# Block 0 of a sliding-window attention layer: output products moved between the score visits, buffers reassigned, one LayerNorm step later

## The chip, the cores and the metric

The kernel runs on one core of a Trainium2 chip. The metric is the device time of one execution in microseconds (us). The core's engines are TensorE (PE in the profile; its weight loads are PEld), VectorE (DVE), ScalarE (ACT), GpSimd (POOL) and SyncE (SP), which here issues the DMAs. Each engine runs its own instructions in order; they meet through semaphores.

## The reference

One layer of a transformer over 2048 rows of 1024 columns, in bf16: a LayerNorm, causal attention with 32 heads of 32 columns in which a query sees itself and the 255 rows ahead of it, an output projection with a residual, a second LayerNorm, and a feed-forward part of width 3584 with a residual.

```python
qkv = (x @ wqkv).reshape(B, S, 3, H, Dh) ...
scores = jnp.einsum("bhqd,bhkd->bhqk", q, k) * (Dh ** -0.5)
mask = (idx[:, None] - idx[None, :] >= 0) & (idx[:, None] - idx[None, :] < W)   # W = 256
p = _softmax(jnp.where(mask[None, None], scores, -1e9), axis=-1)
o = jnp.einsum("bhqk,bhkd->bhqd", p, v) ... @ wo
h = x + _A_ref(_layernorm(x), wqkv, wo)
h2 = h + silu(_layernorm(h) @ w1) @ w2
```

## The kernel before, in words

The rows are cut into four blocks of 512. TensorE's dense work is a list of groups of 8 matmuls of 128 x 512: for each block 8 groups for v and 16 for q and k (four heads share one group of 128 columns), then 32 groups of the output projection (`wo_group`), then the feed-forward part. A group accumulates in one of three PSUM banks taken in turn (`next_acc`; `bank0` to `bank2`), and VectorE (for some early groups ScalarE) copies the result out with one CAST, `L266` for q and k, `L256` for v.

The attention's small work is threaded into this dense work. `Attention.between` is called ahead of every dense matmul and counts them in `seen`; a number such as 108 below is such a position, "the matmul before which something is put". From the first q group of block 0 (position 0) to the end of the output projection the kernel keeps two tables by position:

- A **visit** (`visit_0` for block 0, `visit` for the later ones) is a burst of some 30 to 50 small score matmuls (`L377`). The scores of one unit of four heads go to `sc`, a PSUM tile of four banks. The scores of one to three further heads of neighbouring units go to single banks beside it, which the code calls `idle` (the bank of the next dense group), `out` (the fourth bank, `bank3`) and `behind` (the bank of the dense group before, which must have been copied out by then). ScalarE then takes the exponentials, the single banks first and in the order of the code, `sc` last (`L426` and `L435` in block 0; `L318`, `L324` and `L325` later), and writes them to SBUF; GpSimd zeroes the masked triangles in place (`select`, `L446`), and in block 0 copies one 64-column strip from a unit to its neighbour (`join_0`, `L408`).
- A **piece** (`attn_piece`) is the product of these exponentials with v for two of a group's four heads: 18 matmuls in block 0, 24 later (`L456`), into `bank3`, the same bank that a visit calls `out`. VectorE then divides by the row sums (`attn_norm`: a reciprocal at `L467` and a multiplication at `L468`). After a group's second piece a DMA transpose of the result is put on the SP queue (`attn_transpose`, by `run_late` ahead of the next dense group).

Block 0 has 16 units, numbered m = 2i + odd for group of heads i; piece (i, pair) reads units 2i and 2i+1 for two heads. Its ten visits stand at positions 84, 108, 132, 148, ... 244; from there on a visit of the later blocks stands at every 16th position, 260, 276, 292 and so on. Visits come in threes: the first holds four heads of a unit and three of the next, the second four of a unit and heads of two others, the third four of a unit and the last two heads of its neighbour.

The exponentials of block 0 lie in one SBUF tile, `r_e`, of 13312 columns. A unit needs 2560 columns, 640 a head. There are five places for units: Z (column 0), A (3072), B (5632), C (8192) and D (10752). Later blocks use the same columns: the first 3072 as a ring for the corner chunks (`c_ring`), A and C for `xbuf`, B and D for `ybuf` of even and odd groups. In those a head has 512 columns of triangles and 128 of a middle chunk, the middles of four heads behind the triangles. A place may be written again only after the pieces that read it.

Next to that, VectorE does the first LayerNorm of block 1 while block 0's q and k groups run, as a list of steps taken from the front behind each group: four of row statistics, a first guess of the reciprocal root, three Newton rounds (three small instructions each, `L216` to `L218`), then four row-wise normalizations (`L223`) with a DMA transpose (`L227`) for each. How many steps are taken behind which of the 16 groups is a tuple of 16 numbers (line 682). Groups 10 to 15 are copied out by VectorE, so a step behind one group stands ahead of the next group's copy in VectorE's queue. The transposed rows feed block 1's v groups, which begin at position 128.

Lines that the change touches: `POS_0` (41), `chunk_of` (293), `exp_xy` (321), `visit` (332), `visit_0` (410), the tables of `Attention` (485) and the tuple (682).

Of the kernel before, what the change touches and what calls it, by code (L numbers as in the profile page):

```python
# [11 lines left out]
ACT = mybir.ActivationFunctionType  # L12
ALU = mybir.AluOpType

P = 128
# [22 lines left out]
    [(0, "X", 2), (1, "Y", 1), (2, "X", 3)],  # L38
    [(1, "Y", 2), (2, "C", 1), (3, "Y", 3)],
]  # L40
POS_0 = [(0, 3072, 5632, 8192, 10752)["ZABCD".index(c)] for c in "ZDABCDZBADZCADBC"]
PIECE_0 = {"X": (0, 128, 512, 320), "Y": (0, 128, 256, 512)}
FIRST = [
    (0, 0), (1,), (0, 1), (1, 0), (0, 2), (1, 1), (0, 3), (1, 2), (1, 3),
# [5 lines left out]
def kernel(  # L50
# [10 lines left out]
    nc = tc.nc  # L61
# [11 lines left out]
    G = H // 4  # L73
    VW = DH + 1
    scale = float(DH) ** -0.5
# [21 lines left out]
    four = [ps.tile([P, 512], F32, name=f"bank{i}") for i in range(4)]  # L97
# [31 lines left out]
    def xbuf(i):  # L129
        return r_e[:, 3072 + 5120 * (i % 2):5632 + 5120 * (i % 2)]  # L130

    def ybuf(i):
        return r_e[:, 5632 + 5120 * (i % 2):8192 + 5120 * (i % 2)]

    def tri_of(e):
        return e[:, 0:2048].rearrange("p (h c q) -> p h c q", h=4, q=256)

    def full_of(e):
        return e[:, 2048:2560].rearrange("p (h q) -> p h q", q=P)
# [136 lines left out]
    def run_late():  # L276
        while late:
            late.pop(0)()
# [11 lines left out]
            late.append(lambda: nc.sync.dma_start(out=h_dram[(b * 4 + j) * P:(b * 4 + j + 1) * P, :], in_=t_out[j % 2]))  # L290


    def chunk_of(i, bank, piece, h):
        if i >= G and bank == "C":
            return c_ring[:, (i + 1) % 3, h, piece * P:(piece + 1) * P]
        if i >= G:
            c0 = 2048 + h * P if piece == 2 else h * 512 + (piece - piece // 3) * P
        else:
            c0 = POS_0[2 * i + (bank != "X")] + h * 640 + (384 if bank == "C" else PIECE_0[bank][piece])
            return r_e[:, c0:c0 + P]  # L300
        return (xbuf if bank == "X" else ybuf)(i)[:, c0:c0 + P]

    def unit_xy(i, odd):
        q0 = odd * P
        mid, first, last = odd, odd - 2, odd + 2
        return [
            [(i, mid, q0, q0 + 320, 64), (i, last, q0 + 256, q0 + 384, 384), (i, first, q0, q0 + 64, 0)],
            [(i, mid, q0 + 64, q0 + 384, 128), (i, first, q0, q0 + 128, 0), (i, last, q0 + 320, q0 + 384, 448)],
        ]

    def unit_c(i):
        pair = (i, i + 1) if (i + 1) % 3 < (i + 2) % 3 else (i + 1, i)
        return [[(ii, kt, q * P, q * P + P, (n * 2 + m) * P)
                 for n, ii in enumerate(pair) for m, (kt, q) in enumerate(((-1, 0), (2, 3)))]] * 2

    def exp_c(i, h, bank):
        lo, hi = sorted(((i + 1) % 3, (i + 2) % 3))
        nc.scalar.activation(out=c_ring[:, lo:hi + 1:hi - lo, h, :], in_=four[bank].rearrange("p (n q) -> p n q", q=256),  # L318
                             func=ACT.Exp, scale=scale)

    def exp_xy(e, banks, h0, h1):
        tri, mid = banks[:, :, 0:192], banks[:, :, 192:320]
        tri = bass.AP(tensor=tri.tensor, offset=tri.offset, ap=[*tri.ap[:2], [320, 2], tri.ap[2]])
        nc.scalar.activation(out=tri_of(e)[:, h0:h1, :, 64:256], in_=tri, func=ACT.Exp, scale=scale)  # L324
        nc.scalar.activation(out=full_of(e)[:, h0:h1, :], in_=mid, func=ACT.Exp, scale=scale)  # L325

    def select_xy(e, pair):
        four_q = e[:, 1024 * pair:1024 * (pair + 1)].rearrange("p (c q) -> p c q", q=256)
# [3 lines left out]
    def visit(i, n):  # L332


        now = acc_n[0] % 3
        idle, behind, out = (now + 1) % 3, (now + 2) % 3, 3
        if n == 0:
            own, e_own = unit_xy(i, 0), xbuf(i)
            more = [(0, idle, unit_c(i)), (1, out, unit_c(i)), (2, behind, unit_c(i))]
        elif n == 1:  # L340
            own, e_own = unit_xy(i, 1), ybuf(i)
            more = [(3, idle, unit_c(i)), (0, out, unit_xy(i + 1, 0)), (1, behind, unit_xy(i + 1, 0))]
        else:
            own, e_own = unit_xy(i + 1, 1), ybuf(i + 1)
            more = [(2, out, unit_xy(i + 1, 0)), (3, behind, unit_xy(i + 1, 0))]
        scores(own, more, {idle, out} if n == 0 else ())
        side = [h for h, _, unit in more if len(unit[0]) == 3]
        for h, bank, unit in more:
            if h in side:
                exp_xy(xbuf(i + 1), four[bank].rearrange("p (h q) -> p h q", h=1), h, h + 1)  # L350
            else:
                exp_c(i, h, bank)
        if side:
            select_xy(xbuf(i + 1), side[0] // 2)
        exp_xy(e_own, sc[:], 0, 4)
        for pair in range(2):
            select_xy(e_own, pair)
# [34 lines left out]
    def heads_0(m, h0, h1):  # L392
        return r_e[:, POS_0[m] + 640 * h0:POS_0[m] + 640 * h1].rearrange("p (h q) -> p h q", q=640)

    def select_0(m, h0, h1):
        e = heads_0(m, h0, h1)

        if m % 2:
            select(e[:, :, 0:P], e[:, :, 0:P], True)
            select(e[:, :, 512:640], e[:, :, 320:448], True)  # L400
            select(e[:, :, 256:384], e[:, :, 256:384], False)
        else:
            select(e[:, :, 512:640], e[:, :, 256:384], False)
            select(e[:, :, 0:P], e[:, :, 0:P], True)
            select(e[:, :, 320:448], e[:, :, 320:448], True)

    def join_0(m, h0, h1):
        nc.gpsimd.tensor_copy(out=heads_0(m, h0, h1)[:, :, 384:448], in_=heads_0(m - 1, h0, h1)[:, :, 448:512])  # L408

    def visit_0(k):  # L410

        now = acc_n[0] % 3
        idle, behind, out = (now + 1) % 3, (now + 2) % 3, 3
        m, n = k // 3 * 5, k % 3
        if k == 9:
            own, more = m, []
        elif n == 0:
            own, more = m, [(0, idle, m + 1), (1, out, m + 1), (2, behind, m + 1)]
        elif n == 1:
            own, more = m + 2, [(3, idle, m + 1), (0, out, m + 3), (1, behind, m + 3)]  # L420
        else:
            own, more = m + 4, [(2, out, m + 3), (3, behind, m + 3)]
        scores(unit_0(own), [(h, bank, unit_0(mm)) for h, bank, mm in more], (idle, out))
        for h, bank, mm in more:
            at = POS_0[mm] + 640 * h
            nc.scalar.activation(out=r_e[:, at:at + 512], in_=four[bank], func=ACT.Exp, scale=scale)  # L426
        done = []
        for mm in sorted({mm for _, _, mm in more}):
            heads = [h for h, _, x in more if x == mm]
            if mm % 2:  # L430
                done.append((mm, heads[0], heads[-1] + 1))
                select_0(*done[-1])
            elif heads[-1] == 3:
                select_0(mm, 0, 4)
        nc.scalar.activation(out=heads_0(own, 0, 4)[:, :, 0:512], in_=sc[:], func=ACT.Exp, scale=scale)  # L435
        step = 2 if own % 2 else 4
        for h in range(0, 4, step):
            select_0(own, h, h + step)
            if own % 2:
                join_0(own, h, h + step)  # L440
        for mm, h0, h1 in done:
            join_0(mm, h0, h1)
# [42 lines left out]
    class Attention:  # L485


        def __init__(self):
            self.seen = 0
            self.visits, self.pieces = {}, {}  # L490
            at = [84, 108, *range(132, 260, 16)]
            for k in range(10):
                self.visits[at[k]] = lambda k=k: visit_0(k)
            gaps = (1, 6), (2, 6), (2, 10), (3, 7), (4, 6), (4, 10), (5, 6), (5, 10), (6, 6), (6, 10), (7, 7), (8, 6), (8, 10), (9, 7)
            for d, (k, late) in enumerate(gaps):
                self.pieces[at[k] + late] = (d // 2, d % 2)
            self.pieces.update({267: (G - 1, 0), 271: (G - 1, 1)})
            for p in range((NB - 1) * G // 2):
                i, t = G + 2 * p, 256 + 48 * p
                for n in range(3):  # L500
                    self.visits[t + 4 + 16 * n] = lambda i=i, n=n: visit(i, n)
                for n in range(4):
                    self.pieces[t + (41, 46, 59, 76)[n]] = (i + n // 2, n % 2)
# [87 lines left out]
    for n, step in enumerate(FIRST):  # L591
# [24 lines left out]
        elif len(step) == 4:  # L616
            j, k0, k1, _ = step
# [10 lines left out]
    for j in range(2):  # L628
        for c in range(2):
            nc.scalar.activation(out=v[:, j, c * 16:(c + 1) * 16, 0:DH], in_=first[j][c].rearrange("p (h d) -> p h d", d=DH),  # L630
                                 func=ACT.Identity, scale=rs[:, j:j + 1])
# [44 lines left out]
    for g0 in range(0, G, 4):  # L676
        for w in range(2):
            for g in range(g0, g0 + 4):
                run_late()
                n = g0 * 2 + w * 4 + g % 4  # L680
                qk_group(0, w, g, dve if g % 2 or n > 9 else act, stream.between)
                for _ in range((0, 0, 0, 0, 0, 0, 1, 1, 1, 1, 2, 1, 2, 3, 3, 1)[n]):
                    steps.pop(0)()
    assert not steps

# [166 lines left out]
```

## Time and profile before

| | |
|---|---|
| median of 3 runs | 689.88 us (689.15 to 690.59) |
| the profiled execution | 688.68 us, of which the profile's span is 687.0 us |
| PE busy | 673.2 us, 98% of the span |
| DVE, ACT, POOL busy | 296.0, 235.7, 160.9 us |
| granted clock of PE | 1.0 throughout |

The profile's timeline has one row for consecutive instructions of one engine and kind: start, duration, engine, line, operation, output <- input, size and count, and in brackets the idle time of that engine ahead of it with what ended it. Two things help in reading it. Some matmul records are missing; a gap of one dense step (0.216 us) behind a visit is often such a record. And the end of a matmul is modelled, so it is best to go by starts.

### The profile page before, as it was taken

The page shows a single profiled execution, that of the slowest core. Times are in us where ns is not written, and L with a number is a line of the kernel's source. Part 1 is how long each engine was busy: PE and PEld are TensorE (multiplying, and loading weights), DVE is VectorE, ACT ScalarE, POOL GpSimd, SP SyncE. Part 2 cuts the span into 40 slices and gives each one's busy share as a digit, 9 for nine tenths or more (in the row PEclk, how much of TensorE's full clock was granted, in tenths as well). Part 3 has the DMA queues.
Part 4 walks back from the last instruction along what each step waited for, and adds up shares of the span by engine and source line. Part 5 has one row for each costly group of instructions (what it writes and reads, how often), then busy time and mean ns, then how long its engine had stood idle before and what let it go on. Part 6 is the DMA issues. An engine that isn't in the chain of part 4 may idle for free.

```text
span 687.0 us, 14482 instructions
## 1 busy us (share of the span) xinstructions
PE 673.2 (98%) x6097; PEld 338.0 (49%) x6200; DVE 296.0 (43%) x617; ACT 235.7 (34%) x397; POOL 160.9 (23%) x287
## 2 busy tenths in 40 slices
PE   9999999999999999999999999999999999999998
PEld 4445555555555555444444444444444444444445
DVE  5296755774444446743316133342244251343111
ACT  7346666676767674023300033200133100233000
POOL 1046867666676755000000000000000000000000
PEclk9999999999999999999999999999999999999999
DMA  8824144125522788775033310023300123100110
GB/s 275 260 43 107 18 71 94 26 31 109 181 80 71 209 275 224 152 252 188 1 98 110 77 39 1 0 93 77 76 1 0 36 85 87 39 1 0 31 38 24
DMA packets 77616, 61.49 MB, mean 90 GB/s; under 512 B 52464, under 2 KB 60656, under 8 KB 77552
## 3 DMA queue, kind: packets, MB, share of 16 engines
q1 hardware_dynamic: 77408, 60.31, 32.0%
q8 instruction: 48, 0.79, 0.5%
q10 hardware_dynamic: 144, 0.26, 0.1%
q14 instruction: 16, 0.13, 0.1%
HBM read 39.85 MB, written 8.39 MB: 70 GB/s over the span
## 4 chain that ended last, share of the span: by engine, by line
PE 97%; issue 2%; DVE 1%; ACT 0%; ACTq 0%
PE hacc L771 16%; PE hacc L799 15%; PE bank L264 15%; PE bank L799 13%; PE bank L771 12%; PE bank L285 8%; PE bank L254 6%; PE bank L456 5%; PE sc L377 2%; PE bank L377 2%; PE bank L588 1%; PE tp L254 1%; PE bank L188 0%; ACT r_e L324 0%; DVE r_a L266 0%
## 5 line engine op out<-in xcount | busy, mean ns | idle before, releaser
L446 POOL TENSOR_SCALAR_AFFINE_SELECT r_e<-r_e 128x512 bf16<-128x512 bf16 (+2 forms) x264 | 154.3, 598 | 108.6 <-ACT r_e L324 50.8
L799 PEld LDWEIGHTS <-r_a 128*128 128x128 bf16 x952 | 90.8, 98 | 103.0
L771 PEld LDWEIGHTS <-r_w 128*128 128x128 bf16 x896 | 87.6, 98 | 105.8
L799 PE MATMUL hacc<-r_a 128*128 128x512 bf16 (+2 forms) x523 | 103.2, 357 | 0.5
L799 PE MATMUL bank<-r_a 128*128 128x512 bf16 x411 | 91.3, 380 | 0.5
L771 PE MATMUL hacc<-r_e,r_w 128*128 128x512 bf16 x374 | 84.3, 380 | 0.5
L264 PEld LDWEIGHTS <-r_w 128*128 128x128 bf16 x512 | 45.3, 97 | 47.8
L771 PE MATMUL bank<-r_e,r_w 128*128 128x512 bf16 x286 | 64.3, 380 | 0.1
L266 DVE CAST r_a<-bank 128x512 bf16<-128x512 f32 x59 | 40.7, 689 | 48.6 <-PE bank L264 38.9
L264 PE MATMUL bank<-r_t,r_w 128*128 128x512 bf16 x233 | 57.6, 379 | 2.5 <-issue 1.9
L264 PE MATMUL bank<-r_w 128*128 128x512 bf16 x241 | 56.2, 379 | 1.9 <-issue 1.6
L285 PE MATMUL bank<-r_o,r_a 128*128 128x512 bf16 x242 | 56.5, 379 | 1.5 <-issue 1.1
L324 ACT ACTIVATE r_e<-sc 128x1536 bf16<-128x1536 f32 x36 | 53.5, 1485 | 0.0
L456 PEld LDWEIGHTS <-r_e 128*128 128x128 bf16 x1440 | 45.6, 96 | 15.8 <-issue 1.4
L780 ACT ACTIVATE r_n<-bank 128x512 f32<-128x512 f32 x18 | 10.7, 597 | 117.0 <-PE bank L771 117.0
L456 PE MATMUL bank<-r_a,r_e 128*128 128x33 bf16 x1440 | 46.2, 178 | 0.1
L318 ACT ACTIVATE r_e<-bank 128x512 bf16<-128x512 f32 x48 | 26.1, 598 | 43.5 <-PE bank L377 43.5
L780 ACT ACTIVATE r_n<-hacc 128x512 f32<-128x512 f32 x24 | 14.3, 597 | 75.5 <-PE hacc L771 75.5
L814 DVE SCALAR_TENSOR_TENSOR r_t<-bank,r_t 128x512 bf16<-128x512 f32 x15 | 10.3, 685 | 66.6 <-PE bank L799 66.6
L285 PEld LDWEIGHTS <-r_a 128*128 128x128 bf16 x256 | 23.4, 97 | 25.7
L814 DVE SCALAR_TENSOR_TENSOR r_t<-hacc,r_t 128x512 bf16<-128x512 f32 (+2 forms) x19 | 12.0, 633 | 53.8 <-PE hacc L799 48.4
L377 PEld LDWEIGHTS <-r_a 32*64 32x64 bf16 x1856 | 23.9, 104 | 20.8 <-issue 20.0
(98 smaller groups left out, 592.8 us busy)
## 6 DMA issues: line engine op xcount, KB each, us to landing
r_w<-in_B_w_dram SPq DMA_DIRECT2D x8, 896.0 KB, 6.1
r_a<-in_B_w_dram SPq DMA_DIRECT2D x7, 1024.0 KB, 9.9
r_w<-in_A_wqkv_dram SPq DMA_DIRECT2D x4, 1024.0 KB, 8.5
h_dram<-r_t SPq DMA_DIRECT2D x16, 256.0 KB, 2.9
r_t<-h_dram SPq DMA_DIRECT2D x16, 256.0 KB, 3.0
out_dram<-r_t SPq DMA_DIRECT2D x31, 128.0 KB, 1.7
r_e<-h_dram SPq DMA_DIRECT2D x3, 1024.0 KB, 5.8
r_o<-in_A_x_dram SPq DMA_DIRECT2D x11, 256.0 KB, 5.3
```

What stands on the lines that cost most here:

```text
L254: nc.tensor.matmul(acc, lhsT=lnT_b[b % 2][:, kt, j * P:(j + 1) * P], rhs=wv[:, kt, c * 512:(c + 1) * 512], start=(kt == 0), stop=(kt == KT ...
L264: nc.tensor.matmul(acc, lhsT=wqk[:, kt, col0:col0 + P], rhs=lnT_b[b % 2][:, kt, :], start=(kt == 0), stop=(kt == KT - 1))
L266: copy(out=(qT, kT)[which][b][:, g, :], in_=acc)
L285: nc.tensor.matmul(acc, lhsT=qT[b][:, g, j * P:(j + 1) * P], rhs=wo[:, g, c * 512:(c + 1) * 512], start=(g == 0), stop=(g == G - 1))
L318: nc.scalar.activation(out=c_ring[:, lo:hi + 1:hi - lo, h, :], in_=four[bank].rearrange("p (n q) -> p n q", q=256), func=ACT.Exp, scale=scale)
L324: nc.scalar.activation(out=tri_of(e)[:, h0:h1, :, 64:256], in_=tri, func=ACT.Exp, scale=scale)
L377: nc.tensor.matmul(bank[half * 64:half * 64 + 64, col:col + qb - qa], lhsT=kT[t // 4][r0:r0 + DH, g, k0:k0 + 64], rhs=qT[b][r0:r0 + DH, g, ...
L446: nc.gpsimd.affine_select(out=dst, in_=src, pattern=[[0, n] for n in dst.shape[1:-1]] + [[sgn, P]], compare_op=ALU.is_ge if upper else ALU ...
L456: nc.tensor.matmul(o_ps[:, qt * 2 + hh, 0:VW], lhsT=chunk_of(i, bank, piece, pair * 2 + hh), rhs=v[:, b * 4 + kt, g * 4 + pair * 2 + hh, : ...
L771: nc.tensor.matmul(acc, lhsT=w1[:, kt, ft * P:(ft + 1) * P], rhs=ln2T[b][:, kt, :], start=(kt == 0), stop=(kt == KT - 1))
L780: nc.scalar.activation(out=th, in_=acc, func=ACT.Tanh, scale=0.5)
L799: nc.tensor.matmul(acc[:, 0:c1 - c0], lhsT=gT[:, ft, j * P:(j + 1) * P], rhs=w2[ft // 4][:, ft % 4, c0:c1], start=(ft == 0), stop=(ft == F ...
```

## The change

Three things move.

1. **Pieces.** Block 0's pieces get new positions. A visit that is followed by two pieces now has them 5 and 10 positions behind it (before: 6 and 10). The two pieces of group 5, which stood behind two different visits (219 and 234), now both stand behind the visit at 212 (217 and 222); group 6's first piece goes from 238 to 235. The last piece of block 0 goes from 271 to 284, behind the visit at 276. Three others move by one position.
2. **Buffers.** So that these positions find their data and do not overwrite it, units 10, 12, 13, 14 and 15 change places: 10 from Z to B, 12 from A to Z, 13 from D to A, 15 from C to D, and 14 from B to a new place N at column 7936, which covers the end of B and most of C. Since unit 14's last two heads are now still to be read when the visit at 276 has written its exponentials, the middle chunks of an odd group's `xbuf` are stored with heads 2 and 3 first (`mid_at`): what the visit at 276 writes then lies clear of them. In `visit_0`, the join of a unit whose neighbour was finished by an earlier visit is issued directly behind its selects, and no longer behind the selects of the visit's own unit.
3. **Newton rounds.** The tuple of steps takes none behind group 11 and three behind group 12 (before: one and two), so the second of the three Newton rounds moves from behind group 11's copy to behind group 12's.

```diff
-POS_0 = [(0, 3072, 5632, 8192, 10752)["ZABCD".index(c)] for c in "ZDABCDZBADZCADBC"]
+POS_0 = [(0, 3072, 5632, 7936, 8192, 10752)["ZABNCD".index(c)] for c in "ZDABCDZBADBCZAND"]
...
+    def mid_at(i, bank, h):
+        return (h + 2) % 4 if bank == "X" and i % 2 else h
...
-            c0 = 2048 + h * P if piece == 2 else h * 512 + (piece - piece // 3) * P
+            c0 = 2048 + mid_at(i, bank, h) * P if piece == 2 else h * 512 + (piece - piece // 3) * P
...
-    def exp_xy(e, banks, h0, h1):
+    def exp_xy(e, banks, h0, h1, m0=0):
...
-        nc.scalar.activation(out=full_of(e)[:, h0:h1, :], in_=mid, func=ACT.Exp, scale=scale)
+        nc.scalar.activation(out=full_of(e)[:, m0:m0 + h1 - h0, :], in_=mid, func=ACT.Exp, scale=scale)
...
-                exp_xy(xbuf(i + 1), four[bank].rearrange("p (h q) -> p h q", h=1), h, h + 1)
+                exp_xy(xbuf(i + 1), four[bank].rearrange("p (h q) -> p h q", h=1), h, h + 1, mid_at(i + 1, "X", h))
...
-                done.append((mm, heads[0], heads[-1] + 1))
-                select_0(*done[-1])
+                select_0(mm, heads[0], heads[-1] + 1)
+                if own == mm - 1:
+                    done.append((mm, heads[0], heads[-1] + 1))
+                else:
+                    join_0(mm, heads[0], heads[-1] + 1)
...
-            gaps = (1, 6), (2, 6), (2, 10), (3, 7), (4, 6), (4, 10), (5, 6), (5, 10), (6, 6), (6, 10), (7, 7), (8, 6), (8, 10), (9, 7)
+            gaps = (1, 7), (2, 5), (2, 10), (3, 7), (4, 5), (4, 10), (5, 5), (5, 10), (6, 5), (6, 10), (7, 5), (7, 10), (8, 7), (9, 7)
...
-            self.pieces.update({267: (G - 1, 0), 271: (G - 1, 1)})
+            self.pieces.update({267: (G - 1, 0), 284: (G - 1, 1)})
...
-                for _ in range((0, 0, 0, 0, 0, 0, 1, 1, 1, 1, 2, 1, 2, 3, 3, 1)[n]):
+                for _ in range((0, 0, 0, 0, 0, 0, 1, 1, 1, 1, 2, 0, 3, 3, 3, 1)[n]):
```

## The prediction, made blind

> **What bounds the kernel.** I read the page first, then busy time by stretch, then the timeline around block 0's visits.
>
> ```profile
> span 687.0 us, 14482 instructions
> PE 97%; issue 2%; DVE 1%; ACT 0%; ACTq 0%
> ```
> ```profile
> 38.40:112.00 73.60, 71.18 (x1126) 39.51 (x1145) 49.73 (x116) 44.61 (x59) 49.86 (x108) 1.00 0.35 66
> ```
> ```profile
> 326.77 6.91 PE hacc L771 x32
> ```
>
> The first two are the page's span and the shares of the chain that ended last: PE carries it. The third is the stretch of the visits concerned (38.4 to 112 us; columns: length, then busy time and count of PE, PEld, DVE, ACT, POOL, then clock): PE is idle for 2.4 of 73.6 us, and DVE, ACT and POOL are busy for about 60 to 70%. So nothing but PE can be the bound in the mean, and all that a reordering can win here are the moments in which PE waits. The fourth, from the chain, is the undisturbed dense rate: 6.91 / 32 = 0.216 us a step. I use it as a ruler: a place where starts lie further apart than the work between them is a stall. With it I find four kinds.
>
> **Stall 1: the visit at 108.** The timeline around it, and the visit at 212, which has the same make-up:
>
> ```profile
> 43.84 0.15 DVE L216 SCALAR_TENSOR_TENSOR ln_t<-rs_a,ln_var 128x4 f32<-128x4 f32 x1
> 44.02 0.48 DVE L217 TENSOR_TENSOR ln_t<-ln_t,rs_a 128x4 f32<-128x4 f32 x1
> 44.54 0.26 DVE L218 SCALAR_TENSOR_TENSOR rs_a<-ln_t,rs_a 128x4 f32<-128x4 f32 x1
> 44.72 0.68 DVE L266 CAST r_a<-bank 128x512 bf16<-128x512 f32 x1
> 45.32 0.15 DVE L216 SCALAR_TENSOR_TENSOR ln_t<-rs_a,ln_var 128x4 f32<-128x4 f32 x1
> 45.50 0.16 DVE L217 TENSOR_TENSOR ln_t<-ln_t,rs_a 128x4 f32<-128x4 f32 x1
> 45.70 0.16 DVE L218 SCALAR_TENSOR_TENSOR rs_a<-ln_t,rs_a 128x4 f32<-128x4 f32 x1
> 45.90 0.55 DVE L223 TENSOR_SCALAR r_o<-r_o,st_a,rs_a 128x1024 bf16<-128x1024 bf16 x1
> ```
> ```profile
> 44.60 0.35 PE L377 MATMUL bank<-r_a 32*64 32x320 bf16 x2
> 45.45 0.35 PE L377 MATMUL bank<-r_a 32*64 32x320 bf16 x2 [0.28 <-DVE r_a L266]
> 46.02 0.38 PE L264 MATMUL bank<-r_w 128*128 128x512 bf16 x1 [0.16 <-issue]
> ...
> 76.75 0.35 PE L377 MATMUL bank<-r_a 32*64 32x320 bf16 x2
> 77.56 0.59 PE L264 MATMUL bank<-r_t,r_w 128*128 128x512 bf16 x2 [0.16 <-issue]
> ```
>
> Part of the visit's scores go to the bank of group 12, and that bank is copied out at 44.72 to 45.40, behind the Newton round at 43.84 to 44.80. PE waits within the visit. From the visit's first matmul to the next recorded dense one it takes 46.02 - 44.60 = 1.42 us, the undisturbed one 77.56 - 76.75 = 0.81: the stall is 0.61 us, more than the 0.28 in brackets, because modelled ends cover part of it.
>
> The change puts this round behind group 12's copy. The copy can then start at 43.84, where the round started, and ends near 44.5, ahead of the visit. I count **-0.61**. What is now late is the rest: two rounds and the first normalization stand behind that copy. In the rows a round takes 0.54 (45.32 to 45.86) or 0.96 (43.84 to 44.80). From 44.44 on, two rounds and 0.55 end between 46.07 and 46.91, against 46.45 before.
>
> Queued behind them is group 13's copy (its bank is wanted three groups later) and, on SP, the first DMA transpose of the normalized rows. From the transposes' view of this stretch, and PE's first matmul that reads them:
>
> ```profile
> DMA to landing us min/median/max: 3.2/3.3/4.9
> ```
> ```profile
> 50.58 0.38 PE L254 MATMUL bank<-r_w,r_t 128*128 128x512 bf16 x1
> ```
>
> It can be issued at 46.45 and lands 3.2 us later, at 49.65; it is first read at 50.58, which becomes 49.97. With the bounds it would land between 49.3 and 50.1: the wait is 0 to 0.15. I take 0, for this reason: the slow round ran beside GpSimd, and GpSimd then pauses:
>
> ```profile
> 44.44 0.34 POOL L408 COPY r_e<-r_e 128x192 bf16<-128x192 bf16 x1
> 45.80 0.29 POOL L446 TENSOR_SCALAR_AFFINE_SELECT r_e<-r_e 128x128 bf16<-128x128 bf16 x1 [1.02 <-ACT r_e L426]
> ```
>
> From 44.78 to 45.80 GpSimd is idle, so one round and most of the other meet no GpSimd work. [...]
>
> **Stall 2: the second piece of a pair.** The first and the last of six pairs (behind 132, 164, 180, 196, 228 and 260):
>
> ```profile
> 53.42 0.61 PE L456 MATMUL bank<-r_a,r_e 128*128 128x33 bf16 x18
> 53.87 1.02 PE L254 MATMUL bank<-r_w,r_t 128*128 128x512 bf16 x4
> 54.85 0.61 PE L456 MATMUL bank<-r_a,r_e 128*128 128x33 bf16 x18
> ...
> 93.47 1.02 PE L264 MATMUL bank<-r_t,r_w 128*128 128x512 bf16 x4
> 94.44 0.61 PE L456 MATMUL bank<-r_a,r_e 128*128 128x33 bf16 x18
> ```
> ```profile
> 54.38 0.42 DVE L468 TENSOR_TENSOR r_n<-bank,recip 128x256 bf16<-128x256 f32 x1
> ```
>
> Four steps behind 53.87 the second piece should start at 54.73; it starts at 54.85, 0.05 after the multiplication that frees `bank3` (54.80). The last pair: 94.33 due, 94.44 seen. So 0.115 us a pair. Five steps in place of four leave 0.10 us to spare, and the last pair is split up. 6 x 0.115 = **-0.69**.
>
> **Stall 3: the visits at 276 and 292.**
>
> ```profile
> 95.68 0.68 DVE L266 CAST r_a<-bank 128x512 bf16<-128x512 f32 x1
> 96.07 0.61 PEld L377 LDWEIGHTS <-r_a 32*64 32x64 bf16 x44 [0.42 <-issue]
> 96.76 0.39 PE L264 MATMUL bank<-r_t,r_w 128*128 128x512 bf16 x1
> 99.77 0.66 ACT L325 ACTIVATE r_e<-sc 128x512 bf16<-128x512 f32 x1
> 100.31 0.32 PEld L377 LDWEIGHTS <-r_a 32*64 32x64 bf16 x16 [0.42 <-issue]
> 100.48 0.34 PE L377 MATMUL sc<-r_a 32*64 32x320 bf16 x8
> ...
> 110.60 0.43 PE L377 MATMUL sc<-r_a 32*64 32x320 bf16 x24
> 111.41 0.38 PE L254 MATMUL bank<-r_w 128*128 128x512 bf16 x1 [0.16 <-issue]
> ```
>
> At 276 the piece just ahead (271) delays the copy of the bank that the visit needs to 96.36; the visit takes 96.76 - 96.07 = 0.69 us against 111.41 - 110.60 - 0.216 (one step's record is missing) = 0.59: 0.10 lost. At 292 weights are loaded at 100.31, but the scores start at 100.48, 0.05 after ScalarE has emptied `sc` (100.43): 0.17 lost, since no piece stood between the two visits. The change takes the piece away from 271 and puts it at 284. Both should go, **-0.10** and **-0.17**: with one piece in it, the way from 276 to 292 is 0.59 + 16 x 0.216 + 0.45 = 4.50 us, and ScalarE needs 100.43 - 96.07 + 0.05 = 4.41. So 0.09 to spare.
>
> **What the change adds.** PE's work is the same, and each moved piece costs its 0.45 us (53.42 to 53.87) wherever it stands. New is that a first piece comes one step sooner behind a visit, where `bank3` must have been read by ScalarE. In three visits (164, 196, 212) that is the second exponential; here are the last two, and the dense restart behind 196:
>
> ```profile
> 72.12 1.08 ACT L426 ACTIVATE r_e<-bank 128x512 bf16<-128x512 f32 x2 [2.34 <-PE bank L377]
> 77.29 1.08 ACT L426 ACTIVATE r_e<-bank 128x512 bf16<-128x512 f32 x2 [1.82 <-PE bank L377]
> ```
> ```profile
> 72.18 1.47 PE L264 MATMUL bank<-r_t,r_w 128*128 128x512 bf16 x6
> ```
>
> The bank is free at 73.20 and 78.37, and PE can go on 0.05 later, by the two wake-ups above: 73.25 and 78.42. Five steps behind the dense restart the piece is due at 73.26 and 78.42 (77.56 less one missing step, plus 1.08). So nothing is lost, but nothing is to spare either. I take **0**. A gain is excluded, since the pieces cost their time anyway; a wake-up of twice to three times the 0.05 would lose up to 0.1 each, 0.3 for the three. [...]
>
> Does the data arrive? The tightest is group 5's second piece at 222, which needs unit 11's last head from the visit at 212:
>
> ```profile
> 77.95 0.90 POOL L446 TENSOR_SCALAR_AFFINE_SELECT r_e<-r_e 128x128 bf16<-128x128 bf16 x3 [0.32 <-ACT r_e L426]
> ```
> ```profile
> 82.45 0.47 POOL L408 COPY r_e<-r_e 128x64 bf16<-128x64 bf16 x2
> ```
>
> Counted from the visit's start (76.75), the selects end at +2.10, and the join, now right behind them, near +2.4. The piece comes at 0.59 + 10 x 0.216 + 0.45 = +3.20. It waits for nothing. The joins moved forward (four of them, 0.24 us each) push the selects behind them back by as much; those are wanted a visit later, so 0.
>
> The transposes of groups 5 and 7 move on the SP queue, the one sooner and the other past two LayerNorm transposes of block 2; all are read tens of us later, so 0. The moved places cost no instruction. Who writes a place anew takes scores that PE issues behind the last piece that read it (the closest: unit 14 by the visit at 228, over what the pieces at 217 and 222 read), so no write waits: 0.
>
> **Sum.** 0.61 + 0.69 + 0.10 + 0.17 = 1.57 us. The profiled execution (688.68 us, 1.2 below the median of the runs) would take 687.1; the median of 689.88 becomes **688.3**, or -0.23%. PE carries 97% of the chain to the end, so what is won early is kept.
>
> **Rivals.**
> - *`bank3` comes late.* The pieces at +5 wait for ScalarE, up to 0.3 us. For: no slack at three of them. Against: the wake-up of 0.05 us is seen twice. It gives 688.5.
> - *The transposed rows come late.* The LayerNorm takes the place of the wait at 108, at 0.15 us: 688.5. For: 0.3 us of slack and rounds that doubled beside GpSimd. Against: its pause.
> - *The visits close up on ScalarE and GpSimd, so that the change does not do what it says.* The stalls of 2 and 3 come back at the next visit, and only the Newton term stays: 689.3. For: slacks of 0.09 and 0.10 us, smaller than one dense step. Against: the first and the last pair lose the same, so these spacings repeat closely.
> - *Slower: the join still comes behind the visit's own selects.* Then the piece at 222 waits until 82.45 + 0.24 + 0.05, which is +5.99 behind the visit, against +3.20: 2.8 us lost for 1.57 won, 691.1. It decides as soon as that join ends later than 4.8 us behind the visit. Against: the new branch issues it at once, unit 10 being an earlier visit's.
>
> **How the numbers follow.** The forecast has 0.62, late `bank3` 0.14, late rows 0.06, closing up 0.14, slower 0.04. The three runs spread by 0.7 us to either side, a median perhaps by 0.4; 0.2% (1.38 us, 688.5) is about what a measurement of this kernel can tell from no change. The forecast lies 0.2 us beyond that line, so some two thirds of its 0.62 (0.41) count as faster, and half of the two rivals at 688.5 (0.10); closing up counts as the same. Faster 0.51, same 0.45, slower 0.04. The range reaches from 687.4 (the forecast less twice the spread of a median) to 689.6 (closing up, plus most of that spread).
>
> **What would show it.** In the profile after: group 12's copy starts near 43.84 and the visit at 108 has no second part; second pieces start 1.53 us behind first ones with no bracket; the scores at 292 start with their weights; the block-1 v groups start near 50.0. The position of everything behind 112 us is earlier by about 1.6. It is wrong if first pieces start later than five steps behind a visit, if v groups wait for the DMA, or if new waits for ACT or POOL stand at visits 212 to 292.

## The result

The changed kernel takes 687.4 us (median of 9 runs, 686.83 to 688.1), the kernel before 689.15 (9 runs, 688.59 to 690.59): ratio 0.997, 95% interval [0.996, 0.998], faster by 0.3%. (The ratios in this document are not the quotients of the two medians; they differ from these by up to 0.0005.) The forecast was 688.3, from a base of 689.88.

The profiled execution took 687.66 us, its span 685.9. From its page: the span, and the chain that ended last.

```profile
span 685.9 us, 14588 instructions
PE 98%; DMA 2%; DVE 0%; issue 0%; SPq 0%; ACT 0%; DVEq 0%
```

PE still bounds the kernel. Of the 2% of DMA, which the first profile of before does not have, half is a store of h near 260 us (1% on the page); it comes back below.

**The visit at 108.** VectorE's rows of the timeline around it, then PE's and, behind the dots, PE's first matmul of block 1's v groups:

```profile
42.94 1.29 DVE L266 CAST r_a<-bank 128x512 bf16<-128x512 f32 x2
44.15 0.33 DVE L216 SCALAR_TENSOR_TENSOR ln_t<-rs_a,ln_var 128x4 f32<-128x4 f32 x1
44.52 0.16 DVE L217 TENSOR_TENSOR ln_t<-ln_t,rs_a 128x4 f32<-128x4 f32 x1
...
45.31 0.16 DVE L218 SCALAR_TENSOR_TENSOR rs_a<-ln_t,rs_a 128x4 f32<-128x4 f32 x1
45.51 0.57 DVE L223 TENSOR_SCALAR r_o<-r_o,st_a,rs_a 128x1024 bf16<-128x1024 bf16 x1
```
```profile
43.99 0.38 PE L264 MATMUL bank<-r_w 128*128 128x512 bf16 x1
44.30 0.35 PE L380 MATMUL bank<-r_a 32*64 32x320 bf16 x2
...
44.88 0.61 PE L264 MATMUL bank<-r_w 128*128 128x512 bf16 x2
...
49.66 0.59 PE L254 MATMUL bank<-r_w,r_t 128*128 128x512 bf16 x2
```

The copies of groups 11 and 12 now run one behind the other and are done at 44.23, ahead of the visit. The visit takes 44.88 - 44.30 = 0.58 us, with no record missing; undisturbed it was 0.81 - 0.216 = 0.59. The two Newton rounds behind the copy take 0.73 us (44.15 to 44.88) and 0.56 (44.91 to 45.47), and the normalization ends at 46.08.

**Pairs, and the visits at 276 and 292.** Two pieces behind the visit at 132; then the visit at 276, ScalarE's last exponential of it, and the visit at 292:

```profile
52.29 0.61 PE L462 MATMUL bank<-r_a,r_e 128*128 128x33 bf16 x18
52.74 1.24 PE L254 MATMUL bank<-r_w,r_t 128*128 128x512 bf16 x5
53.82 0.61 PE L462 MATMUL bank<-r_a,r_e 128*128 128x33 bf16 x18
...
94.00 0.54 PEld L380 LDWEIGHTS <-r_a 32*64 32x64 bf16 x44 [0.42 <-issue]
94.59 0.39 PE L264 MATMUL bank<-r_t,r_w 128*128 128x512 bf16 x1
97.61 0.66 ACT L328 ACTIVATE r_e<-sc 128x512 bf16<-128x512 f32 x1
98.61 0.52 PEld L380 LDWEIGHTS <-r_a 32*64 32x64 bf16 x36 [0.42 <-issue]
98.61 0.43 PE L380 MATMUL sc<-r_a 32*64 32x320 bf16 x24
```

The second piece starts 53.82 - 52.74 = 1.08 us behind the dense restart, five steps of 0.216: no stall. The other pairs show the same: in the first profile of before the second piece starts 1.43 or 1.44 us behind the first in all six (0.45 + 4 x 0.216 = 1.31 was due), in the changed kernel 1.53 or 1.54 in all five that are left (0.45 + 5 x 0.216 = 1.53). (Beside the pieces whose moves the list of the change names, only one moves by one position, from 114 to 115, and not three.) The visit at 276 takes 0.59, and at 292 weights and scores start together, 0.34 us after `sc` is free.

**Where the 1.57 us can be read, and what scatters.** I cut each profiled execution at three visits: the first one (position 84), the one at 324, and the last one near 262. The times are differences of the starts of their first score matmul:

| profile | start to visit 84 | 84 to 324 | 324 to last visit | last visit to end | span |
|---|---|---|---|---|---|
| before | 38.74 | 71.86 | 153.43 | 422.94 | 687.0 |
| before, second | 39.09 | 71.86 | 153.43 | 423.65 | 688.0 |
| before, third | 38.53 | 71.85 | 153.42 | 423.68 | 687.5 |
| changed | 38.44 | 70.29 | 153.90 | 423.32 | 685.9 |
| changed, second | 38.98 | 70.29 | 153.43 | 423.20 | 685.9 |
| changed, third | 39.17 | 70.29 | 153.42 | 423.32 | 686.2 |

The column from 84 to 324 holds everything the change touches. It is the same to 0.01 us in every execution of a kernel, and it fell by 1.57 us. The other columns scatter by up to 0.7 us between executions of one kernel; that is why single spans (687.0 against 685.9) show only 1.1 of it. Why the first visit starts at 38.4 in one execution and at 39.2 in another stays open.

The last column's scatter has a cause in the trace. In the changed kernel, VectorE at the end of the attention, then PE's last visit and the dense matmul behind it:

```profile
256.65 0.69 DVE L287 TENSOR_TENSOR r_t<-bank,r_a 128x512 bf16<-128x512 f32 x1 [0.35 <-PE bank L285]
261.34 0.69 DVE L287 TENSOR_TENSOR r_t<-bank,r_a 128x512 bf16<-128x512 f32 x1 [3.99 <-DMA h_dram<-r_t]
...
262.52 0.68 DVE L287 TENSOR_TENSOR r_t<-bank,r_a 128x512 bf16<-128x512 f32 x1
```
```profile
262.63 0.43 PE L380 MATMUL sc<-r_a 32*64 32x320 bf16 x24
...
263.59 0.39 PE L285 MATMUL bank<-r_o,r_a 128*128 128x512 bf16 x1
```

An addition of the output projection waits for one of two buffers (`t_out`) until the store of h from it has landed. The addition behind it ends at 263.20, and the last visit (262.63) needs the bank that it reads: the visit takes 263.59 - 262.63 = 0.96 us, some 0.38 more than undisturbed. The store was issued at 253.9 and landed 7.3 us later. In the first profile of before this wait is 2.7 us long and PE loses nothing; in the second and third, PE loses 0.7. The addition in the first, with a row of ScalarE ahead of it that is needed further down:

```profile
261.55 1.50 ACT L324 ACTIVATE r_e<-sc 128x1536 bf16<-128x1536 f32 x1
...
261.88 0.69 DVE L287 TENSOR_TENSOR r_t<-bank,r_a 128x512 bf16<-128x512 f32 x1 [2.67 <-DMA h_dram<-r_t]
```

### The profile page after: what moved, and what is told of

It reads as the page before. It is cut to its first block, busy times and chain, and to the rows that moved or that the text cites. A ratio compares the mean times of both kernels' runs of the same rounds, so it can differ in the third digit from the quotient of the medians.

```text
span 685.9 us, 14588 instructions
## 1 busy us (share of the span) xinstructions
PE 681.7 (99%) x6200; PEld 337.6 (49%) x6200; DVE 295.5 (43%) x617; ACT 235.7 (34%) x397; POOL 161.3 (24%) x287
## 4 chain that ended last, share of the span: by engine, by line
PE 98%; DMA 2%; DVE 0%; issue 0%; SPq 0%; ACT 0%; DVEq 0%
PE bank L264 17%; PE hacc L777 16%; PE hacc L805 15%; PE bank L805 13%; PE bank L777 12%; PE bank L285 7%; PE bank L254 7%; PE bank L462 5%; PE sc L380 2%; PE bank L380 2%; DMA h_dram<-r_t 1%; PE bank L594 1%; PE tp L254 1%; DMA r_o<-in_A_x_dram 0%; PE tp L546 0%
## 5 line engine op out<-in xcount | busy, mean ns | idle before, releaser
L264 PE MATMUL bank<-r_t,r_w 128*128 128x512 bf16 x256 | 61.9, 379 | 0.0
L264 PE MATMUL bank<-r_w 128*128 128x512 bf16 x256 | 59.2, 379 | 0.0
L285 PE MATMUL bank<-r_o,r_a 128*128 128x512 bf16 x256 | 58.9, 379 | 0.0
```

The source lines that it names most:

```text
L264: nc.tensor.matmul(acc, lhsT=wqk[:, kt, col0:col0 + P], rhs=lnT_b[b % 2][:, kt, :], start=(kt == 0), stop=(kt == KT - 1))
L285: nc.tensor.matmul(acc, lhsT=qT[b][:, g, j * P:(j + 1) * P], rhs=wo[:, g, c * 512:(c + 1) * 512], start=(g == 0), stop=(g == G - 1))
```

## The experiments

Times are medians, taken in three series, each on one chip and beside runs of the kernel before. First series: before 689.25 (33 runs).

**Newton round alone** (the tuple on the kernel before):

```diff
-(0, 0, 0, 0, 0, 0, 1, 1, 1, 1, 2, 1, 2, 3, 3, 1)[n]
+(0, 0, 0, 0, 0, 0, 1, 1, 1, 1, 2, 0, 3, 3, 3, 1)[n]
```

> The kernel before with the Newton round moved and nothing else. If the stalls on PE add up one by one, the visit at 108 loses its second part and takes 0.81 us or less from its first matmul to the next recorded dense one (1.42 before), everything behind it comes 0.61 us earlier, the second pieces of pairs still start 0.115 us late, and the time falls by about 0.6 us (ratio 0.9991). Rival, the gain in block 0 is given back where the output projection waits for DMAs (around 261 us of the changed kernel's trace): the profile shows 0.6 us won at 112 us and part of it lost again between 255 and 265 us, and the time falls by 0.0 to 0.4 us.

Measured: 688.73 us, 0.52 below before, ratio 0.9997 [0.9988, 1.0006]. In the profile the way from 84 to 324 is 71.24 us, 0.62 less. At the last visit 0.30 us is lost to the store of h. The mechanism and its size are shown by the profile; by the times alone it can't be told from nothing.

**Pieces, buffers and joins without the Newton round** (that tuple put back in the changed kernel).

> The changed kernel with the Newton round back in its old place, so pieces, buffers and joins alone. If the stalls add up: the visit at 108 stalls for 0.61 us as before, six second pieces each win 0.115, the visits at 276 and 292 win 0.10 and 0.17, together 0.96 us at the first visit behind 300, and the time falls by about 1.0 us (ratio 0.9986). Rival as in the other run, lost again between 255 and 265 us: 0.1 to 0.7 us.

Measured: 688.39 us, 0.86 below before, ratio 0.9991 [0.9983, 1.0]. From 84 to 324: 70.90, 0.96 less, and the stall at 108 is there again (PE again waits 0.3 us for VectorE's copy). 0.62 + 0.96 = 1.58: the two halves add up to the whole (1.57).

**The last piece back at 271.**

```diff
-self.pieces.update({267: (G - 1, 0), 284: (G - 1, 1)})
+self.pieces.update({267: (G - 1, 0), 271: (G - 1, 1)})
```

> The changed kernel with the last piece of block 0 back at 271 and nothing else undone. By the prediction's terms the piece at 271 starts 0.115 us late again, the visit at 276 takes 0.10 us longer, and the scores at 292 wait 0.17 us for ScalarE: 0.385 us in the profile, and 0.1 to 0.4 in the time. Rival, the shorter way between 260 and 292 is made up by the next visits: nothing at the visit at 308.

Measured in the second series (before 689.21, 27 runs): 688.22 us, ratio 0.9982 [0.9973, 0.9992]. From 84 to 324: 70.67, 0.38 more than the changed kernel. Its timeline has the old picture again:

```profile
92.17 1.02 PE L264 MATMUL bank<-r_t,r_w 128*128 128x512 bf16 x4
93.15 0.61 PE L462 MATMUL bank<-r_a,r_e 128*128 128x33 bf16 x18
...
94.38 0.68 DVE L266 CAST r_a<-bank 128x512 bf16<-128x512 f32 x1
94.78 0.61 PEld L380 LDWEIGHTS <-r_a 32*64 32x64 bf16 x44 [0.42 <-issue]
95.47 3.63 PE L264 MATMUL bank<-r_t,r_w 128*128 128x512 bf16 x16
98.48 0.65 ACT L328 ACTIVATE r_e<-sc 128x512 bf16<-128x512 f32 x1
99.02 0.68 PEld L380 LDWEIGHTS <-r_a 32*64 32x64 bf16 x36 [0.42 <-issue]
99.19 0.43 PE L380 MATMUL sc<-r_a 32*64 32x320 bf16 x24
```

0.12 at the second piece, 0.10 within the visit at 276 (0.69 against 0.59), 0.17 between weights and scores at 292. So each of the three terms is the piece's position, one by one.

**First pieces at +4** behind the visits at 164, 196 and 212: `(4, 5), (6, 5), (7, 5)` become `(4, 4), (6, 4), (7, 4)`.

> The changed kernel with the first piece four and not five positions behind the visits at 164, 196 and 212. The prediction said that at five positions there is neither a wait for bank3 nor any slack. If so, each of these pieces starts where it started before, 0.22 us later than the dense steps would let it, and costs 0.67 us in place of 0.455: 0.64 us in all. If instead the bank was free sooner (slack the prediction did not see), the pieces start one step sooner and the three together cost less than 0.3 us.

Measured: 688.20 us, ratio 0.9982 [0.9973, 0.9991]; from 84 to 324 70.88, 0.59 more than the changed kernel. Behind the visit at 196:

```profile
71.79 1.57 ACT L429 ACTIVATE r_e<-bank 128x512 bf16<-128x512 f32 x3 [2.23 <-PE bank L380]
71.84 1.04 PE L264 MATMUL bank<-r_t,r_w 128*128 128x512 bf16 x4
...
72.92 0.60 PE L462 MATMUL bank<-r_a,r_e 128*128 128x33 bf16 x18
```

Four steps behind 71.84 the piece was due at 72.70 and started at 72.92, five steps behind. By the 1.08 us that two of these exponentials take in the prediction's rows, ScalarE has read the bank at 72.87, 0.05 sooner. At 164, 196 and 212 the pieces start 1.05, 1.08 and 1.09 us behind the dense restart (four steps are 0.86, five 1.08). So the bank is free just in time for position 5: no wait there, and next to no slack, as predicted.

**Joins put back** (in `visit_0`, always the old order):

```diff
-                if own == mm - 1:
+                if True:
```

> The changed kernel with every join of a unit's second half put back behind the selects of the visit's own unit, as in the kernel before. The rival that ended slower said that the piece at 222 then waits for the join at 5.99 us behind the start of the visit at 212, against 3.20 due: 2.8 us lost, so about 1.2 us slower than before and 2.6 us slower than the changed kernel. Against it, if ScalarE or GpSimd get to that join sooner than in the trace of before: the piece waits less, and the time lies between the changed kernel's and before's. The other three joins put back should cost nothing.

Measured: 691.53 us, ratio 1.0035 [1.0022, 1.0049]: slower than before, as that rival said. GpSimd and PE behind the visit at 212 (75.44 here):

```profile
78.65 0.56 PE L462 MATMUL bank<-r_a,r_e 128*128 128x33 bf16 x16
79.39 1.81 POOL L452 TENSOR_SCALAR_AFFINE_SELECT r_e<-r_e 128x512 bf16<-128x512 bf16 x3 [0.53 <-ACT r_e L441]
81.15 0.46 POOL L411 COPY r_e<-r_e 128x64 bf16<-128x64 bf16 x2
...
81.44 0.22 PE L462 MATMUL bank<-r_a,r_e 128*128 128x33 bf16 x2 [2.23 <-POOL r_e L411]
```

The piece starts on time, does the 16 matmuls that don't need the late strip, and waits with the last two until the first of the two joins is done: 2.39 us on the way from 84 to 324 (72.68 against 70.29), in place of 2.8, because most of the piece runs ahead of the wait. Nothing else is lost in block 0. That makes 72.68 - 71.86 = 0.82 us against before; with a start 0.24 us sooner (38.50), the first profile's 688.68 becomes 689.26, which is what this profiled execution took. The four other runs took 691.46 to 692.95, at a mean granted clock of 0.997 to 0.998 where every other run of the study had 1.0. 0.2 to 0.3% of 690 us is 1.4 to 2.1 us; by this estimate the lower clock goes with a good part of the 2.2 to 3.7 us that these four took above the profiled execution. No run of another kernel has a lower clock. That the stop of over 2 us on PE brought it down is my guess from that, and not shown: the profiled execution has the stop too, at 1.0, and the four have no profile.

**The store of h.** The changed kernel with two of the w1 loads later:

```diff
-        if n in (1, 3, 5, 7, 13):
-            load_w1((1, 3, 5, 7, 13).index(n))
+        if n in (1, 3, 5, 13, 17):
+            load_w1((1, 3, 5, 13, 17).index(n))
```

> The changed kernel with two loads of w1 (0.9 MB each) issued later in the output projection: behind its groups 1, 3, 5, 13 and 17 in place of 1, 3, 5, 7 and 13. In the changed kernel's trace VectorE waits 3.99 us until 261.2 for a store of h that was issued at 253.9 behind such loads, PE loses 0.38 us at the visit that follows, and a further 0.48 us inside the piece at 259.7 that no wait in the profile explains. If full DMA queues are behind both, the store lands some 3 us sooner, both losses go, and the time is 0.4 to 0.9 us below that of the changed kernel in the same call. Rival, the two losses are chance in one execution: no difference beyond 0.2 us between the two.

> The changed kernel unchanged, profiled once more and timed beside the others. If the waits are structural, the profile again shows no stall from 38 to 112 us, 1.57 us won there, and a loss of 0.3 to 0.9 us between 255 and 265 us; the time is 1.0 to 1.8 us below before. If the loss at 255 to 265 us was chance, it is missing or elsewhere this time.

Measured: 687.21 us with the later loads (ratio 0.9974 [0.9965, 0.9983]) and 687.84 for the changed kernel (0.9979 [0.997, 0.9987]). With the later loads nothing is lost at the last visit (last visit to end: 422.95 us), without them 0.26.

The same edit on the kernel before, in the second series:

> The kernel before with the same two loads of w1 issued later (behind groups 1, 3, 5, 13 and 17 of the output projection). If the kernel before hides its wait for the store of h, as its profile says (VectorE waits 2.67 us, no stall on PE), the time stays within 0.3 us of before, and the store is no longer waited for. If in other executions before lost time there too, it gains 0.3 to 0.7 us, as the changed kernel did with this edit.

Measured: 688.61 us against 689.21, ratio 0.9989 [0.998, 0.9998]; last visit to end 422.94. So the kernel before gains 0.60, about as much as the changed kernel (0.63). My theory that the change itself had turned part of its gain into this wait falls: before pays it too. That its first profile lost nothing there was chance, as two more showed:

> The kernel before, profiled once more. Its runs have a median near 689.2 us and the profiled execution took 688.68. If the difference is the wait for the store of h near 261 us, this profile (where it is slower than 688.68) shows a loss of 0.2 to 0.6 us at the visit near 264 us; if it is the start, the first visit stands later than 38.74 us and nothing is lost at 264.

> The kernel before, a third profile, for the same question. Sum of the two theories: span = 687.0 + (start later than 38.74) + (loss at the visit near 264).

Measured: spans of 688.0 and 687.5. In the second profile, VectorE's row and the view of the stores issued between 256 and 257 us:

```profile
263.41 0.69 DVE L287 TENSOR_TENSOR r_t<-bank,r_a 128x512 bf16<-128x512 f32 x1 [3.85 <-ACT r_e L324]
```
```profile
L290 SPq DMA_DIRECT2D h_dram<-r_t x1: 811/811/811, 256.4 to 256.4; - x1
DMA to landing us min/median/max: 6.9/6.9/6.9
```

The bracket names ScalarE, whose exponential of `sc` had just ended. But the addition does not depend on it: in the first profile of before it starts in the midst of that same exponential (261.88, in 261.55 to 263.05). The wait ends some 0.15 us after the store landed (256.36 + 6.9 = 263.26), and 0.12 after it in the changed kernel's first profile. 0.71 and 0.74 us are lost at the last visit. Both theories hold: the starts (39.09, 38.53) and this wait together give the spans.

The third series (before 689.06, 12 runs) repeated the comparison:

> The changed kernel beside the one with later loads of w1, timed on the same chip. The change is worth 1.4 to 1.75 us against before, and the later loads a further 0.6: this one 1.3 to 1.8 us below before.

> The changed kernel with the later loads of w1 (behind groups 1, 3, 5, 13 and 17), once more. If its gain is real: 0.4 to 0.8 us below the changed kernel in the same call, about 2.0 us below before, and again no wait for the store of h near 261 us. Rival, scatter: within 0.2 us of the changed kernel.

Measured: the changed kernel 687.40 us (0.9972 [0.9961, 0.9983]), with the later loads 687.13 (0.9968 [0.9956, 0.998]), spans 686.2 and 685.1. In the second, the store takes 5.7 us, and the addition that needs the buffer starts at 259.26, 2.93 us ahead of the last visit (262.19), against 1.31 in the changed kernel beside it:

```profile
259.26 0.69 DVE L287 TENSOR_TENSOR r_t<-bank,r_a 128x512 bf16<-128x512 f32 x1 [1.89 <-ACT r_e L327]
```
```profile
DMA to landing us min/median/max: 5.7/5.7/5.7
```

VectorE is idle for 1.89 us ahead of it, and for 1.78 in the two other profiles with the later loads; so the store, which landed at 259.19, may still have cost 0.1 here. With the loads in the old place it is 2.67 to 3.99 us in all eleven profiles.

The three profiles with the later loads lose nothing at the last visit (422.94 or 422.95 us to the end). Of the eleven with the loads in the old place, three lose nothing and eight lose 0.26 to 0.74 us. What PE loses goes by how long ahead of the last visit's start the store has landed: with the later loads 3.0 to 3.9 us, nothing lost; in the old place 1.9 to 2.3 us, nothing; 1.4 to 1.6 us, 0.26 to 0.41; 1.1 us, 0.71 and 0.74. So the loss goes with the landing, and with the later loads the store landed early enough each time. In the times the gain is less sure: over the changed kernel it is 0.63 and 0.27 us in the two series, with intervals that overlap, so its size stays loose. The changed kernel with the later loads is the fastest version in both.

## Why the prediction was right or wrong

- *Stall 1 (-0.61)*: right, 0.62 measured alone. The reason for taking the transposes' wait as 0 held too: all of the two rounds but the first instruction (0.33 us) ran beside an idle GpSimd (idle from 44.47 to 45.50) and they were short, 0.16 us for each of the other five instructions, where before the `L217` at 44.02 took 0.48 beside GpSimd's selects (42.67 to 44.49); and the v groups started at 49.66 without a wait. The first transpose was issued at 46.1, behind the normalization's end at 46.08, and landed 3.2 us later, some 0.3 us ahead of that read.
- *Stall 2 (-0.69) and 3 (-0.10, -0.17)*: right. Putting the last piece back returned 0.38 us, and its three parts (0.12, 0.10, 0.17) are the predicted terms; the rest of 0.96 is 0.58, the five other pairs at 0.115 each, which the traces show one by one.
- *What the change adds (0)*: right, and the slack really is next to zero, as the pieces at +4 showed. The rival of a late `bank3` does not occur.
- *The sum (1.57)*: 1.57 in every profile of the changed kernel. In the times 1.75, 1.41 and 1.66 us, in the result and in the first and third series.
- *The time (688.3) was wrong*, and the step that failed is "the median of 689.88 becomes 688.3": the base. Three runs gave 689.88; the medians of 9, 33, 27 and 12 runs of the same kernel were 689.15, 689.25, 689.21 and 689.06. The term that was mis-sized is "a median perhaps by 0.4": it was 0.7 off. From 689.15 the same sum gives 687.6, against 687.4 measured. The range, hung on the same base, had its lower end at 687.4, so the result lies on its very edge. I had seen that the profiled execution was 1.2 us below the median and did not draw on it.
- *"What is won early is kept"* was argued from the chain's 97% and missed a wait that stood in the profile of before (VectorE, 2.7 us, for the store of h) with PE's next need right behind it. It cost 0.3 to 0.7 us in five of the six profiles of the two kernels. Since it costs before as much, it hardly changed the difference.
- *The rival that visits close up* did not occur. The slack behind a first piece was the predicted 0.10 us, and that was enough, since the way from 84 to 324 repeats to 0.01 us. At 292 it was larger than the predicted 0.09: `sc` was free 0.34 us ahead of the scores, 0.29 with the wake-up of 0.05 (100.43 to 100.48 in the rows of before). The way from 276 to 292 took 98.61 - 94.00 = 4.61 us and not 4.50, mostly because a visit starts 0.31 us behind the last dense matmul (43.99 to 44.30) and the sum had one step, 0.216; and ScalarE needed 98.27 - 94.00 + 0.05 = 4.32 and not 4.41, since the visit at 276 was shorter.
- *The slower rival* was right in direction and place; 2.8 was too much by the part of the piece that does not need the strip, and the lower clock in four of its five runs was not foreseen.

## What to carry to other kernels

Where one engine carries the chain, read its stalls as start-to-start distances against an undisturbed stretch, and look at which instruction of another engine ends just ahead of the late start; here four such distances, added up, gave the gain to 0.01 us. Take the base for an absolute forecast from all that is known of the kernel's scatter, the profiled execution included, and not from a median of three. And when work in front is shortened, look also at waits on other engines that are hidden today by a few tenths of a us: here they cost 0.26 to 0.74 us in eight of the eleven profiles with the w1 loads in the old place.

## What the runs showed that I had not expected

- Four of five runs of the kernel with the late joins, in which PE stops for 2.4 us, had a mean granted clock of 0.997 to 0.998 and took 691.46 to 692.95 us, against 689.26 at 1.0. No run shows where the clock fell, since the profiled execution was the fifth: whether the stop did it stays open.
- In eleven of fourteen profiles VectorE sits idle for 2.7 to 4.0 us until a store of h has landed. It cost PE nothing as long as the store had landed 1.9 us ahead of the last visit, and up to 0.74 us where it landed later; with two w1 loads of 0.9 MB issued later, one of which had stood ahead of the store, it landed 3.0 to 3.9 us ahead.
- In one profile of the changed kernel PE stopped for 0.48 us inside a piece, with no wait shown:

```profile
259.73 0.54 PE L462 MATMUL bank<-r_a,r_e 128*128 128x33 bf16 x15
260.57 0.40 PE L462 MATMUL bank<-r_a,r_e 128*128 128x33 bf16 x9 [0.30 <-issue]
```

It is the 153.90 in the table, did not come again in the two further profiles, and its cause stays open.
